# Four 128-row loads of wo in place of sixteen, and the last z1 load queued behind the fourth output store

## The chip, the cores and the metric

The kernel runs on one core of a Trainium2 chip. The metric is the device time of one execution in microseconds. Three runs of the kernel before gave 616.48, 617.76 and 618.69 us, with 617.76 us as the median.

## The reference

The input x (2048 tokens by 512 channels) goes through a layer norm without scale or shift. Two branches read the result, and x and both branches are added:

```
xn  = layernorm(x)
q, k, v = xn @ wqkv                      # 32 heads of 16
phi(t) = [softmax(t @ w_phi), softmax(-t @ w_phi)]
kv  = phi(k)^T v;  z = sum of phi(k) over the tokens
o   = phi(q) kv / (phi(q) z + 1e-6)      # linear attention
A   = o @ wo                             # wo is 512 x 512
z1, z2 = gelu(xn @ w_in) in two halves of 688 columns
g   = w_sp @ layernorm(z2) + b_sp        # w_sp is 2048 x 2048
B   = (z1 * g) @ w_out
out = x + A + B
```

## The kernel before

The tokens are split into 16 tiles of 128. Each product in full precision is made of three matrix multiplies: every operand is held as a rounded part (`_h`) and a rest (`_l`), and `mm3` (lines 55 to 59) issues high by high, high by low and low by high. A weight that comes from DRAM therefore passes two engines before it can be used: ACT rounds it (`round_h`, line 49) and DVE subtracts (`rest_l`, line 53).

The program has three stages. The first makes q, k, v, the softmax features and raw z1, and sends features (`e_d`) and raw z1 (`z1_d`) to DRAM. The second is the large product w_sp by layernorm(z2) (tiles `g`), two output tiles at a time; after each pair, `gate` multiplies by gelu(z1), turns the result on DVE and stores it (`u_d`, `ur_d`). The third, "the tail", is the loop of lines 1076 to 1104. For each pair of token tiles it does, on PE:

- `project_u` (line 1012): the gated tile `uh`, `ul` and its last rows `rt` times w_out, into `pout`;
- `attend` (line 995): the features `f` times `kvT`, into `po`; ACT and DVE then make the two parts of `oT` from `po`;
- `project_o` (line 1021): `oT` times wo (`woh`, `wol`), added into the same `pout`. ACT copies `pout` to `xr` (line 1040) and an accumulating store on POOL's queue adds it to `out` (line 1041);
- `attend_T` (line 976): for the pairs up to token tile 6, sixteen transposes on PE (line 989, into `ptq`) turn the features of the next pair; later pairs are turned by DVE and sent through DRAM (`q_d`).

`features(s)` normalises the features of tile s on DVE (`q_fin`, lines 564 to 571): a multiply and a reduce of 1,024 columns, four short instructions, and a second multiply of 1,024 columns on the tile `et`, which SP loads from `e_d` (line 557). The transposes for the pair (2, 3) need `features(2)` and `features(3)`.

The order around the change is that of the program as a scheduler laid it out. Each engine runs its instructions in order; a transfer is issued by an engine's queue in order too. SP's queue carries, before the tail: the features of the first pair (`f`, line 923), the gated tile 1 (`u`, lines 855 and 856), `kvT` (line 972), wo (line 850), then `et` of tile 3, the gated tiles 2 and 3 (`u`, `rt`), `et` of tile 4, and so on. POOL's queue carries the z1 loads (line 787), the stores of gated tiles (`u_d`, `ur_d`, lines 837 and 839), the feature stores (`q_d`, line 582; `qtmp` is their source in the tail) and the output stores. The queue instructions take their completion semaphores from a ring of eight, so that a load waits until the load eight places ahead of it on its queue has landed.

wo is used in an order of rows that suits `oT`: chunk c of 128 rows consists of four blocks of 32 rows, each 64 rows apart in DRAM. The kernel before loads the four blocks with four transfers:

```
    def load_w(src, parts, h, l, t):
        rows = 0
        for r0, r1 in parts:
            load_w.last = sp.dma_start(t[rows:rows + r1 - r0], src[r0:r1, :]).ins
            rows += r1 - r0
        return round_h(act, h, t[:rows]), rest_l(l, t[:rows], h)
```

The z1 of the last pair of tiles (14 and 15) is loaded at line 1097, in the turn i = 2 of the tail's loop, and is used by ACT's gelu (line 819) in the turn i = 6.

Of the kernel before, what the change touches and what calls it, by code (L numbers as in the profile page):

```python
# [10 lines left out]
F32 = mybir.dt.float32  # L11
F32R = mybir.dt.float32r
AF = mybir.ActivationFunctionType
ALU = mybir.AluOpType
# [4 lines left out]
P = 128  # L19
S, D, H, DH, FH = 2048, 512, 32, 16, 688  # L20
# [5 lines left out]
KF = FH // P  # L26
# [8 lines left out]
HP, QP = P // 2, P // 4  # L35
# [6 lines left out]
def mixer(ctx: ExitStack, tc: tile.TileContext, x, x_t, wv, wqkT, phi_bd, wo, w_in, wst, b_r, w_out, out):  # L42
    nc = tc.nc
    pe, act, dve, pool, sp = nc.tensor, nc.scalar, nc.vector, nc.gpsimd, nc.sync


    def round_h(eng, h, src):
        if eng is act:
            return act.activation(h, src, AF.Copy).ins  # L49
        return eng.tensor_copy(h, src).ins  # L50

    def rest_l(l, src, h, eng=None):
        return (eng or dve).tensor_tensor(l, src, h.bitcast(F32), op=ALU.subtract).ins  # L53

    def mm3(dst, a, b, start, stop):
        (ah, al), (bh, bl) = a, b
        pe.matmul(dst, ah, bh, start=start, stop=False)  # L57
        pe.matmul(dst, ah, bl, start=False, stop=False)  # L58
        return pe.matmul(dst, al, bh, start=False, stop=stop).ins  # L59
# [12 lines left out]
    def xz_tile(n, dt, name):  # L72
        return xz.tile([P, SL], dt, tag="xz", name=name)[:, :n]
# [121 lines left out]
    with ExitStack() as p0:  # L195
# [236 lines left out]
        t = xz_tile(2 * D, F32R, "xT").rearrange("p (a b) -> p a b", a=2)  # L432
# [8 lines left out]
        for cs, pt in zip(halves, pts):  # L441
            src = pt.rearrange("p a b -> p (a b)")
# [117 lines left out]
    def q_fin(et, tmp, zb):  # L560

        e, r, t, w = et[:, :NF], *(et[:, NF + k * 2 * H:NF + (k + 1) * 2 * H] for k in range(3))
        den = et[:, NF + 6 * H:QW]
        dve.tensor_tensor(tmp, e, zb, op=ALU.mult)
        dve.tensor_reduce(t, heads(tmp), axis=AX.X, op=ALU.add)
        dve.tensor_tensor(t, t, r, op=ALU.mult)
        dve.scalar_tensor_tensor(den, pairs(t, 0), EPS_DEN, pairs(t, 1), op0=ALU.add, op1=ALU.add)
        dve.reciprocal(den, den)
        dve.tensor_tensor(w.rearrange("p (h a) -> p h a", a=2), r.rearrange("p (h a) -> p h a", a=2),
                          den.unsqueeze(2).to_broadcast([P, H, 2]), op=ALU.mult)  # L570
        return e, dve.tensor_tensor(heads(e), heads(e), bc(w, 2 * H), op=ALU.mult).ins
# [6 lines left out]
    def turn_q(s, dst, e, eng):  # L578

        dve.transpose(dst.rearrange("p (m c t) -> p m c t", c=NB, t=BL), e.rearrange("p (c m j) -> p m c j", c=NB, j=BL))  # L580
        for b in range(P // BL):
            eng.dma_start(q_d[s, :, b * QB:(b + 1) * QB].rearrange("(m j) w -> j m w", j=BL),
                          dst[b * BL:(b + 1) * BL].rearrange("p (m w) -> p m w", w=QB))
# [154 lines left out]
    for s in range(NT):  # L738
# [4 lines left out]
        n = s // 2  # L743
# [3 lines left out]
        for k, q in p:  # L747
            ins = act.activation(z[(slice(None), *k)], q, AF.Gelu_apprx_tanh, scale=r_x[:, s:s + 1]).ins
# [6 lines left out]
        r = zw.tile([P, 1], F32, tag="rstd", bufs=2, name="rstd")  # L755
# [88 lines left out]
    def slot(name, dt=F32):  # L844
        return xz_tile(2 * FH, dt, name)

    def load_w(src, parts, h, l, t):
        rows = 0
        for r0, r1 in parts:
            load_w.last = sp.dma_start(t[rows:rows + r1 - r0], src[r0:r1, :]).ins  # L850
            rows += r1 - r0
        return round_h(act, h, t[:rows]), rest_l(l, t[:rows], h)

    def load_u(i, u, rt):
# [19 lines left out]
    lasts, wu = [None] * 9, []  # L874

    def stage_w():
        t = [xz2.tile([P, SL], F32, tag="b", name="wof") for _ in range(3)]
        w = [xz_tile(2 * D, F32R, "wu") for _ in range(KF + 1)]
        for c in range(KF + 1):
            n = P if c < KF else 2 * REM  # L880
            h, l = (w[c][:n, k * D:(k + 1) * D] for k in range(2))
            rows = [(c * P, (c + 1) * P)] if c < KF else [(KF * P, FH)] * 2
            load_w(w_out, rows, h, l, t[c // 2][:, c % 2 * D:(c % 2 + 1) * D])
            wu.append((h, l))

    g, es, ets, ft, brought = {}, {}, {}, {}, {}
    for n in range(NC):
# [4 lines left out]
        if n % NQ == NQ - 1 and i < NP - 1:  # L892
            c = gt.tile([P, 2, FU], F32, tag="c", name="c")
# [7 lines left out]
        if n % NQ == NQ - 1 and i < NP - 1:  # L901
# [3 lines left out]
            if i in (2, 4):  # L905
                s = i // 2 - 1
                e, t = (gt.tile([P, 2, FU], F32, tag=tag, name=name).rearrange("p k f -> p (k f)")[:, :NF]
                        for tag, name in (("c", "c"), ("z1", "z1t")))
                pool.dma_start(e, e_d[s, :, :NF])
                turn_q(s, t, e, pool)  # L910
        if n == NC - 4:
            stage_w()
# [6 lines left out]
        if n == NC - 2:  # L919
# [4 lines left out]
            t = xz_tile((KF + 1) * P, F32R, "u1")  # L924
# [9 lines left out]
    cw = ctx.enter_context(left("cw", 1))  # L934
# [7 lines left out]
    def er_pair(name):  # L942
        return cw.tile([P, 2, NF], F32, tag="er", bufs=3, name=name)

    def features(s):
        with tc.issue_after(fin[-1]):
            tmp = slot("qtmp")[:, :NF]
            es[s], ins = q_fin(ets.pop(s), tmp, zb)
        fin.append(ins)
        if s >= TQ:  # L950
            if s % 2 == 0:
                ft[s] = er_pair("f")
            turn_q(s, tmp, es.pop(s), pool)
            brought[s] = sp.dma_start(ft[s - s % 2][:, s % 2], q_d[s]).ins
            return
        lasts[6] = ins

    def gated(u):
        return split_u(*u, wk.tile([P, KF, P], F32R, tag="uh", name="uh"), wk.tile([P, KF, P], F32R, tag="ul", name="ul"))
# [2 lines left out]
    wo_h = cw.tile([P, ND, D], F32R, name="woh")  # L962
# [4 lines left out]
    wo_l = cw.tile([P, ND, D], F32R, name="wol")  # L967
# [53 lines left out]
    def project_o(i, oT, p):  # L1021
        ts = slice(i % 2 * P, (i % 2 + 1) * P)
        rows = slice(i * P, (i + 1) * P)
        xr = wk.tile([P, D], F32, tag="xr", bufs=3, name="xr")
        if i >= NT - 2:
            sp.dma_start(xr, x[rows, :])
        if i == NT - 1:
            dve.tensor_tensor(xr, p, xr, op=ALU.add)
            parts = [(slice(k * D // 2, (k + 1) * D // 2), pst.tile([P, D // 2], F32, tag="tr", name="pend")) for k in range(2)]
        else:  # L1030
            parts = [(slice(0, D), p)]
        for cs, q in parts:
            for c in range(ND):
                lasts[4] = mm3(q, (oT[0][:, c, ts], oT[1][:, c, ts]), (wo_h[:, c, cs], wo_l[:, c, cs]),
                               q is not p and c == 0, c == ND - 1)
            if i == NT - 2:
                dve.tensor_tensor(xr, p, xr, op=ALU.add)
                sp.dma_start(out[rows, :], xr)
            elif q is p:
                act.activation(xr, p, AF.Copy)  # L1040
                ins = pool.dma_start(out[rows, :], xr, accum_op=ALU.add).ins
                tc.add_manual_dep(ins, seeds[i].name, mybir.DependencyInfo(
                    mybir.DependencyClass.Sync, mybir.DependencyReason.DATA), reason="out holds x")
            else:
                dve.tensor_tensor(xr[:, cs], q, xr[:, cs], op=ALU.add)
                sp.dma_start(out[rows, cs], xr[:, cs])
# [7 lines left out]
    wk.tile([P, NG, 2 * P], F32R, tag="oTh", name="oT")  # L1054
    with tc.issue_after(lasts[0]), tc.issue_after(lasts[1]), tc.issue_after(fin[-1]):
        for c in range(ND):
            rows = [(m * QP, (m + 1) * QP) for m in range(c // 2 * 8 + c % 2, (c // 2 + 1) * 8, 2)]
            load_w(wo, rows, wo_h[:, c], wo_l[:, c], cw.tile([P, D], F32, tag="wof", bufs=4, name="wof"))
    with tc.issue_after(load_w.last):
        ets[3] = load_q(3, slot("et"))  # L1060
        for s in (2, 3):
# [14 lines left out]
    for i in range(0, NT, 2):  # L1076
        p[i] = project_u(i, nxt.pop(i))
        if 0 < i < NT - 2:
            nxt[i + 2] = gated(us.pop(i + 2))
        with tc.issue_after(lasts[2]):  # L1080
            oT = attend(fT)
        with tc.issue_after(lasts[3]):
            p[i + 1] = project_u(i + 1, nxt.pop(i + 1))
        if not i:
            fin.append(lasts[7])
            features(3)
            with tc.issue_after(fin[-1]), tc.issue_after(lasts[8]):
                nxt[2] = gated(us.pop(2))
        if i < NT - 2:
            with tc.issue_after(fin[-1]) if not i else ExitStack():  # L1090
                nxt[i + 3] = gated(us.pop(i + 3))
        for k in range(2):
            project_o(i + k, oT, p.pop(i + k))
            ahead(i + k)
        if i == 2:
            with tc.issue_after(lasts[6]):
                z = load_z1(NP - 1)
        if i == GATE_LAST:
            with tc.issue_after(lasts[0]), tc.issue_after(lasts[1]):
                gate(NP - 1, cb, z, z, gt.tile([P, 2, FU], F32, tag="zt", name="zt"))()  # L1100
            p2.close()
        if i + 2 < NT:
            with tc.issue_after(lasts[4]):
                fT = attend_T(i + 2)
# [33 lines left out]
```

## Time and profile before

| what | value |
|---|---|
| median of three runs | 617.76 us |
| time of the profiled execution | 615.26 us |
| its span, first to last instruction | 613.6 us |
| busy: PE, DVE, ACT, POOL | 606.3, 519.9, 259.9, 132.4 us |
| granted TensorE clock | 1.000 |
| moved by DMA | 107.85 MB, mean 176 GB/s |

The profile comes from one execution, 2.5 us below the median of the three runs; 1.7 us of its time lie outside its span. Times in its rows are microseconds from the start of the span. In a row of a timeline stand start, duration, engine, line, operation, result and operands; square brackets hold how long the engine had been idle and which event ended that. A DMA's "to landing" runs from its issue to its completion. In a row of the DMA queues stand packets, megabytes and the time that the packets took, as a share of 16 DMA engines over the window. In a row of the stretches stand the bounds, then busy times of PE, PEld, DVE, ACT and POOL with their counts, the granted clock, the mean share of the DMA engines, and GB/s.

### The profile page before, as it was taken

What the parts mean: (1) busy time and instruction counts of PE and PEld (TensorE: products, weight loads), DVE (VectorE), ACT (ScalarE), POOL (GpSimd) and SP (SyncE); (2) the same over time, 40 slices, a digit from 0 to 9 for tenths busy, and PEclk for the clock granted to TensorE, in tenths of its full rate; (3) what the DMA queues carried; (4) which work ended last, traced back from release to release, by engine and by line L of the source; (5) the groups of instructions that cost most, each with busy time, mean ns of one, the idle gap of its engine ahead of it and who ended that gap; (6) DMA issues with size and microseconds to landing.
All of it is one profiled execution on the core that took longest, in us unless ns stands there. A gap on an engine that the chain in (4) does not pass through costs nothing.

```text
span 613.6 us, 11385 instructions
## 1 busy us (share of the span) xinstructions
PE 606.3 (99%) x4286; PEld 551.5 (90%) x4286; DVE 519.9 (85%) x930; ACT 259.9 (42%) x414; POOL 132.4 (22%) x231
## 2 busy tenths in 40 slices
PE   8999999999999999999999999999999999999997
PEld 7888888888888999999999999999999978777776
DVE  5999999999988588999989897787779979999932
ACT  5653334423433547887434443332435243332220
POOL 4122232333111014542000002001100131053440
PEclk9999999999999999999999999999999999999999
DMA  8557776666547848001454746455566798599882
GB/s 309 196 135 170 224 174 183 153 161 171 134 120 206 275 155 308 2 1 35 150 135 133 193 100 182 132 158 145 162 179 215 239 312 253 150 293 278 222 221 67
DMA packets 57950, 107.85 MB, mean 176 GB/s; under 512 B 12392, under 2 KB 24552, under 8 KB 57672
## 3 DMA queue, kind: packets, MB, share of 16 engines
q1 hardware_dynamic: 43656, 65.22, 34.5%
q0 software_dynamic: 11936, 36.28, 24.0%
q10 hardware_dynamic: 2304, 5.64, 2.4%
q8 instruction: 33, 0.54, 0.4%
q14 instruction: 21, 0.17, 0.1%
HBM read 66.85 MB, written 35.54 MB: 167 GB/s over the span
## 4 chain that ended last, share of the span: by engine, by line
PE 83%; DVE 6%; DMA 6%; issue 2%; SPq 1%; ACT 1%; POOL 0%; ACTq 0%; DVEq 0%; POOLq 0%
PE g L57 8%; PE g L58 8%; PE g L59 8%; PE proj L58 7%; PE proj L57 7%; PE proj L59 7%; PE zps L58 6%; PE zps L59 6%; PE zps L57 6%; PE pout L57 5%; PE pout L59 5%; PE pout L58 5%; DVE A L53 2%; DMA wf<-in_wst 1%; PE po L1004 1%
## 5 line engine op out<-in xcount | busy, mean ns | idle before, releaser
L57 PE MATMUL g<-B,A 128*128 128x344 f32 x448 | 142.5, 319 | 0.3 <-DVE c L810 0.3
L58 PE MATMUL g<-B,A 128*128 128x344 f32 x448 | 142.4, 319 | 0.0
L59 PE MATMUL g<-B,A 128*128 128x344 f32 x448 | 138.9, 318 | 0.0
L57 PEld LDWEIGHTS g<-B,A 128*128 128x128 f32 x448 | 84.0, 188 | 0.9 <-DVE c L810 0.6
L58 PEld LDWEIGHTS g<-B,A 128*128 128x128 f32 x448 | 84.0, 188 | 0.0
L59 PEld LDWEIGHTS g<-B,A 128*128 128x128 f32 x448 | 83.6, 188 | 0.0
L49 ACT ACTIVATE A<-S 128x512 fp32r<-128x512 f32 x64 | 39.4, 628 | 70.7 <-DVE S L622 52.3
L57 PE MATMUL proj<-wqk_h,xT 128*128 128x512 f32 x128 | 50.1, 391 | 0.0
L59 PE MATMUL proj<-wqk_h,xT 128*128 128x512 f32 x128 | 49.8, 389 | 0.0
L58 PE MATMUL proj<-wqk_l,xT 128*128 128x512 f32 x128 | 49.8, 389 | 0.0
L125 ACT ACTIVATE e<-e,r_x 128x1024 f32<-128x1024 f32 x26 | 29.8, 1149 | 42.3 <-DVE e L124 41.3
L53 DVE TENSOR_TENSOR A<-S,A 128x512 fp32r<-128x512 f32 x64 | 43.0, 684 | 3.0 <-ACT A L49 2.8
L49 ACT ACTIVATE A<-wf 128x512 fp32r<-128x512 f32 (+1 forms) x64 | 32.8, 515 | 28.1 <-DMA wf<-in_wst 15.8
L57 PE MATMUL zps<-w1h,xT 128*128 128x344 f32 (+2 forms) x128 | 40.8, 320 | 0.0
L59 PE MATMUL zps<-w1h,xT 128*128 128x344 f32 (+2 forms) x128 | 40.7, 318 | 0.0
L58 PE MATMUL zps<-w1l,xT 128*128 128x344 f32 (+2 forms) x128 | 40.7, 318 | 0.0
L57 PE MATMUL zps<-w2h,xT 128*128 128x344 f32 (+2 forms) x128 | 40.7, 318 | 0.0
L58 PE MATMUL zps<-w2l,xT 128*128 128x344 f32 (+2 forms) x128 | 40.6, 317 | 0.0
L59 PE MATMUL zps<-w2h,xT 128*128 128x344 f32 (+2 forms) x128 | 40.3, 317 | 0.0
L53 DVE TENSOR_TENSOR A<-wf,A 128x512 fp32r<-128x512 f32 (+1 forms) x64 | 35.1, 550 | 4.1 <-ACT A L49 4.0
L787 POOL DMA_DIRECT2D z1t<-z_d x16 | 8.7, 550 | 132.5 <-DMA wf<-in_wst 98.1
L128 DVE TENSOR_REDUCE sm<-e 128x64 f32<-128x1024 f32 x26 | 31.1, 1199 | 2.5 <-ACT e L125 2.5
(219 smaller groups left out, 1434.4 us busy)
## 6 DMA issues: line engine op xcount, KB each, us to landing
wf<-in_wst SPq DMA_DIRECT2D x64, 256.0 KB, 3.4
e_d<-e POOLq DMA_DIRECT2D x16, 544.0 KB, 5.0
et<-e_d SPq DMA_DIRECT2D x16, 544.0 KB, 7.6
z_d<-z1f ACTq DMA_DIRECT2D x16, 344.0 KB, 3.1
z1t<-z_d POOLq DMA_DIRECT2D x16, 344.0 KB, 4.6
zacc<-e POOLq DMA_DIRECT2D x10, 512.0 KB, 4.8
u<-u_d SPq DMA_DIRECT2D x15, 320.0 KB, 5.8
xt<-in_x SPq DMA_DIRECT2D x16, 256.0 KB, 4.4
```

The costliest lines, as they stand in the source:

```text
L49: return act.activation(h, src, AF.Copy).ins
L53: return (eng or dve).tensor_tensor(l, src, h.bitcast(F32), op=ALU.subtract).ins
L57: pe.matmul(dst, ah, bh, start=start, stop=False)
L58: pe.matmul(dst, ah, bl, start=False, stop=False)
L59: return pe.matmul(dst, al, bh, start=False, stop=stop).ins
L125: softmax_pair.last = less, act.activation(e, e, AF.Exp, scale=scale).ins
L128: dve.tensor_reduce(sm, heads(e), axis=AX.X, op=ALU.add)
L787: pool.dma_start(t[:, k, :FH], z1_d[2 * i + k])
L1004: lasts[3] = pe.matmul(po[r][c * QP:(c + 1) * QP, k], kvT[rows, m // 2, cols], fs[m // 4][rows, m // 2 % 2], start=True, stop=True).ins
```

## The change

`load_w` takes a list of views of DRAM and issues one transfer for each. For wo, the four blocks of a chunk are one view of three dimensions (4 blocks, 32 rows, 512 columns), so that each chunk is one transfer of 128 rows. For w_out the transfers stay what they were. Besides, `lasts[6]`, behind which the last z1 load is put, is now the output store that was issued last and no longer the last instruction of `features`; at that place it is the store of output tile 3, the fourth.

```
-    def load_w(src, parts, h, l, t):
+    def load_w(parts, h, l, t):
         rows = 0
-        for r0, r1 in parts:
-            load_w.last = sp.dma_start(t[rows:rows + r1 - r0], src[r0:r1, :]).ins
-            rows += r1 - r0
+        for src in parts:
+            n = src.size() // D
+            load_w.last = sp.dma_start(t[rows:rows + n], src).ins
+            rows += n
         return round_h(act, h, t[:rows]), rest_l(l, t[:rows], h)
...
-        lasts[6] = ins
...
-                ins = pool.dma_start(out[rows, :], xr, accum_op=ALU.add).ins
+                lasts[6] = ins = pool.dma_start(out[rows, :], xr, accum_op=ALU.add).ins
...
-            rows = [(m * QP, (m + 1) * QP) for m in range(c // 2 * 8 + c % 2, (c // 2 + 1) * 8, 2)]
-            load_w(wo, rows, wo_h[:, c], wo_l[:, c], cw.tile([P, D], F32, tag="wof", bufs=4, name="wof"))
+            rows = wo[c // 2 * D // 2:(c // 2 + 1) * D // 2].rearrange("(m a r) d -> a m r d", a=2, r=QP)[c % 2]
+            load_w([rows], wo_h[:, c], wo_l[:, c], cw.tile([P, D], F32, tag="wof", bufs=4, name="wof"))
```

On SP's queue, ahead of the tail, stood the load of kvT, sixteen loads of wo (the staging tile is `wof`), and then the features of tile 3 and the gated tiles 2 and 3:

```order
L972 DMA kvT<-kvT_d 128x512
L850 DMA wof<-in_wo 32x512 x16
L557 DMA et<-e_d 128x1088
L855 DMA u<-u_d 128x640
L856 DMA rt<-ur_d 96x128
L855 DMA u<-u_d 128x640
L856 DMA rt<-ur_d 96x128
L557 DMA et<-e_d 128x1088
```

The same place now:

```order
L972 DMA kvT<-kvT_d 128x512
L851 DMA wof<-in_wo 128x1x512 x4
L557 DMA et<-e_d 128x1088
L856 DMA u<-u_d 128x640
L857 DMA rt<-ur_d 96x128
L856 DMA u<-u_d 128x640
L857 DMA rt<-ur_d 96x128
L557 DMA et<-e_d 128x1088
```

Twelve issues are gone ahead of the load of `et`; nothing else on SP has changed places here.

On POOL's queue, from the last z1 loads of the second stage to the first output stores of the tail, the order was this (`x6` holds the four loads of two earlier pairs and the two of the last pair):

```order
L787 DMA z1t<-z_d 128x688 x6
L837 DMA u_d<-z1t 32x8x160 x4
L839 DMA ur_d<-z1t 32x6x32 x4
L1041 DMA out<-xr 128x512 x4
L582 DMA q_d<-qtmp 32x4x256 x4
L1041 DMA out<-xr 128x512 x2
L582 DMA q_d<-qtmp 32x4x256 x8
```

The same place now:

```order
L787 DMA z1t<-z_d 128x688 x4
L837 DMA u_d<-z1t 32x8x160 x4
L839 DMA ur_d<-z1t 32x6x32 x4
L1041 DMA out<-xr 128x512 x4
L787 DMA z1t<-z_d 128x688 x2
L1041 DMA out<-xr 128x512
L582 DMA q_d<-qtmp 32x4x256 x4
L1041 DMA out<-xr 128x512
L582 DMA q_d<-qtmp 32x4x256 x8
```

The two loads of the last z1 have moved from ahead of the gated stores to behind the fourth output store, and the fifth output store now stands ahead of the first feature stores. PE's and ACT's orders are the same in both kernels. On DVE, in the tail, some instructions have changed places with their neighbours. The widest such move is at the two rests of `oT` of token tiles 6 and 7, which PE reads in `project_o`; before, both stood behind the last two long instructions of `features`:

```order
L567 SCALAR_TENSOR_TENSOR et<-et 128x32
L568 RECIPROCAL et<-et 128x32
L569 TENSOR_TENSOR et<-et 128x64
L571 TENSOR_TENSOR et<-et 128x1024
L564 TENSOR_TENSOR qtmp<-et,zb 128x1024
L53 TENSOR_TENSOR oT<-po,oT 128x2x256 x2
L580 STREAM_TRANSPOSE qtmp<-et 128x1024
```

The same place now:

```order
L568 RECIPROCAL et<-et 128x32
L569 TENSOR_TENSOR et<-et 128x64
L53 TENSOR_TENSOR oT<-po,oT 128x2x256
L571 TENSOR_TENSOR et<-et 128x1024
L564 TENSOR_TENSOR qtmp<-et,zb 128x1024
L53 TENSOR_TENSOR oT<-po,oT 128x2x256
L580 STREAM_TRANSPOSE qtmp<-et 128x1024
```

The first rest has moved ahead of these two; the second stands behind the same instructions as before.

More of the change, by code (lines that the diff above doesn't have):

```diff
@@ L881, in stage_w @@
             h, l = (w[c][:n, k * D:(k + 1) * D] for k in range(2))
-            rows = [(c * P, (c + 1) * P)] if c < KF else [(KF * P, FH)] * 2
-            load_w(w_out, rows, h, l, t[c // 2][:, c % 2 * D:(c % 2 + 1) * D])
+            rows = [w_out[c * P:(c + 1) * P]] if c < KF else [w_out[KF * P:]] * 2
+            load_w(rows, h, l, t[c // 2][:, c % 2 * D:(c % 2 + 1) * D])
             wu.append((h, l))
```

## The prediction

> **What bounds the kernel now.** I read the page's busy times first, then PE's waits, then the chain of waits around the only long one, then the timelines and DMA queues of that stretch. The page:
>
> ```profile
> span 613.6 us, 11385 instructions
> PE 606.3 (99%) x4286; PEld 551.5 (90%) x4286; DVE 519.9 (85%) x930; ACT 259.9 (42%) x414; POOL 132.4 (22%) x231
> ```
>
> PE is idle for 613.6 - 606.3 = 7.3 us in all, so no change that leaves its work alone can give more. PE's waits from 480 us to the end, where the change lies:
>
> ```profile
> PE ptq L989 <- DVE et L571: 1.0, 1, 1.0
> PE pout L57 <- ACT oT L49: 0.2, 1, 0.2
> PE pout L57 <- DVE c L810: 0.2, 1, 0.2
> ```
>
> The first two are within reach of the change: 1.0 + 0.2 = 1.2 us. Behind them PE has no gap until the last pair; the row of the stretches from 504 us shows 94.5 us busy in 94.5:
>
> ```profile
> 504.00:598.50 94.50, 94.50 (x597) 74.69 (x596) 82.52 (x124) 29.82 (x49) 29.02 (x45) 1.00 0.86 239
> ```
>
> So whatever PE gains or loses before 504 us arrives at the end of the kernel undiminished. The chain of waits shows what the 1.0 us hangs on (columns: start, duration, link):
>
> ```profile
> 480.17 6.96 DMA kvT<-kvT_d
> 487.14 0.31 SPq L850
> ...
> 492.24 6.33 DMA et<-e_d
> 498.58 1.24 DVE qtmp L564
> ...
> 502.24 1.24 DVE et L571
> 503.52 1.53 PE ptq L989 x12
> ```
>
> SP issues the sixteen wo loads one after another, held up by landings of earlier loads, and only then the `et` of tile 3. From its landing DVE needs 498.58 to 503.47 us, that is 4.9 us, and PE starts the remaining twelve transposes 0.05 us later. The other short wait belongs to wo itself, as the timelines of ACT, PE and DVE show:
>
> ```profile
> 495.09 0.63 ACT L49 ACTIVATE woh<-wof 128x512 fp32r<-128x512 f32 x1 [2.63 <-DMA wof<-in_wo]
> 496.26 0.50 PE L57 MATMUL pout<-woh,oT 128*128 128x512 f32 x1 [0.18 <-ACT oT L49]
> 496.36 1.28 DVE L53 TENSOR_TENSOR oT<-po,oT 128x512 fp32r<-128x512 f32 x2
> 501.89 0.60 PE L989 MATMUL ptq<-ident,et 128*128 128x128 f32 x4
> ```
>
> ACT is stuck on the last wo chunk until 495.09 us. Its two roundings of `oT` are queued behind that chunk, and so is PE's first product with wo, 1.17 us later. DVE's two rests of `oT` end at 496.36 + 1.28 = 497.64 us, 2.55 us after the landing, and `features(3)` follows them in DVE's order.
>
> **The change part by part: sixteen issues become four.** SP's row of the timeline:
>
> ```profile
> 480.60 11.54 SPq L850 DMA_DIRECT2D wof<-in_wo  x16
> ```
>
> On SP's queue this ends at 492.1 us. Four issues, each at up to 0.67 us (the longest of the `nm_d` issues quoted below, which also have more than two dimensions), end near 483.3 us, so `et` is issued some 9 us earlier. By itself this would take away the 1.0 us.
>
> **How fast the four loads run.** The source view now has 4 blocks as its outermost dimension; the blocks of before had 32 rows. The trace has one transfer whose outermost dimension is 4, the store of the turned means (`nm_d`, line 332), and here is the window that holds the packets of one such store, with its row by line, beside the page's rows of a 128-row store from ACT:
>
> ```profile
> q1 hardware_dynamic: 20, 0.00, 1.8%
> L332 SPq DMA_DIRECT2D nm_d<-mask x10: 508/529/665, 44.1 to 150.9; - x10
> ...
> q10 hardware_dynamic: 2304, 5.64, 2.4%
> z_d<-z1f ACTq DMA_DIRECT2D x16, 344.0 KB, 3.1
> ```
>
> Sixteen z1 stores leave 2304 packets, 144 each: 128 rows and 16 more. The `nm_d` store moves 4 x 4 runs of 32 floats, 16 packets, and leaves 20: only 4 more. I take the extra packets as one closing packet per DMA engine, so this transfer ran on 4 engines and the z1 stores on 16. The Trainium skill, page "DMA: Bandwidth & Descriptors", section "Why a DMA increments its semaphore by 16 and not by 1", states the rule behind it: a transfer is spread over the largest number up to 16 that divides the slowest dimension of both its sides. By this rule a wo load (4 blocks on one side, 128 partitions on the other) gets 4 engines; the trace agrees for 4 against 4, and no row has 4 against 128. The section "Rules for kernel authors" of the page warns against just such an outermost dimension.
>
> On 4 engines a load of 256 KB puts 65.5 KB on each, and the four loads follow one another on the same engines. The rate of one engine with 2 KB rows comes from two windows, the full queue of 5 to 12 us and the wo loads themselves, 487 to 490 us:
>
> ```profile
> q1 hardware_dynamic: 1407, 2.56, 98.4%
> ...
> q1 hardware_dynamic: 292, 0.39, 40.2%
> ```
>
> That is 2.56 MB in 0.984 x 16 x 7 = 110.2 engine-us, 23.2 KB per us, and 0.39 MB in 0.402 x 16 x 3 = 19.3, 20.2 KB per us. A load thus takes 2.82 to 3.24 us. I take 2.9, nearer the first, because four queued loads look like a full queue: 11.6 us for all (11.3 to 13.0).
>
> **When the wo loads start.** They run on their engines behind kvT, which landed at 487.1 us. Two z1 loads were in its way, and they move off:
>
> ```profile
> 479.41 1.07 POOL L787 DMA_DIRECT2D z1t<-z_d  x2 [23.89 <-DVE ul_rt L53]
> q0 software_dynamic: 160, 0.70, 49.1%
> wf<-in_wst SPq DMA_DIRECT2D x64, 256.0 KB, 3.4
> ```
>
> From 481.5 to 486 us POOL's queue took 49.1% of the engines, 4.5 x 0.491 = 2.2 us on each. Without it kvT lands at 484.9 us; the early end is its issue plus the median of the 64 loads of its size, 480.2 + 3.4 = 483.6. I take 484.2, near the middle.
>
> **What shares the four engines.** The gated stores go out on POOL's queue, between 490.5 and 499.5 us:
>
> ```profile
> q0 software_dynamic: 384, 0.75, 35.3%
> ```
>
> They take 9 x 0.353 = 3.2 us of each engine. About half of that falls before 496 us: 1.6 us (0 to 3.2).
>
> **The sum.** The last chunk lands at L = 484.2 + 11.6 + 1.6 = 497.4 us, where it landed at 495.09. `et` of tile 3, 544 KB over 16 engines, sits behind wo on those four with 34.8 KB, 1.5 to 1.7 us, so it is there by L + 1.7, before DVE is free at L + 2.55. The remaining transposes then start at L + 2.55 + 4.9 + 0.05 = L + 7.5, against 503.5 before. Equality lies at L = 496.0; at 497.4 the kernel loses 1.4 us. PE's wait for the first wo product grows from 0.2 to 497.4 + 1.17 - 496.08 = 2.5 us, and the one at the transposes shrinks to about 0.1. For L below 494.8 us both waits are gone, and the gain is 1.2 us and no more.
>
> **The z1 loads** cost nothing where they now stand:
>
> ```profile
> 520.53 0.86 POOL L1041 DMA_DIRECT2D out<-xr  x1 [0.78 <-ACT xr L1040]
> 535.84 0.60 POOL L582 DMA_DIRECT2D q_d<-qtmp  x1 [14.45 <-DVE qtmp L580]
> z1t<-z_d POOLq DMA_DIRECT2D x16, 344.0 KB, 4.6
> 546.53 1.34 ACT L819 ACTIVATE z1t<-z1t 128x1376 f32<-128x1376 f32 x1
> ```
>
> Issued behind the fourth output store, from about 521.4 us, two loads of 4.6 us have landed by 532, even if one waits for the other; gelu reads them at 546.5. POOL is idle there for 14.45 us, so nothing queues behind them. If that cover of 14 us were gone, gelu and the last gate would come later by what is missing. The fifth output store ahead of the first `q_d` store delays the latter by 0.9 us at most; POOL was waiting for DVE there. On DVE the second rest of `oT`, on which PE depends last, stands behind the same work as before, so the exchanged neighbours count nothing.
>
> **The rivals.** *All 16 engines carry the loads.* If the 128 partitions decide the spread, each load puts 16.4 KB on an engine and takes 0.7 us at 23.2 KB per us, and wo is there by 484.9 + 2.8 = 487.7 us. Both waits vanish: 1.2 us gained, 616.5 us. For it speaks that the destination has 128 rows; against it, the 20 packets. The same section of rules in the Trainium skill also advises joining loads under 64 KB into larger ones, and says such loads are mostly overhead; here the 64 KB loads of wo land in 2.0 to 5.4 us by their row, and 256 KB loads in 3.4, which agrees, if all engines take part:
>
> ```profile
> DMA to landing us min/median/max: 2.0/3.1/5.4
> ```
>
> *The gated stores take full turns on the four engines.* The mechanism is mine, its place the queues of these engines from 490 us: if kvT lands at its late end, 484.9, and all 3.2 us of POOL's packets come ahead of the last chunk, L = 484.9 + 11.6 + 3.2 = 499.7 and the loss is 3.7 us: 621.5. It decides from L = 497.9 on, where the loss passes 1.85 us. For it speaks that POOL issues these stores from 490.0 us on, while the wo loads are still running; against it, that a part of them lands later, the last issued ones at 494 + 5.8 = 500 us:
>
> ```profile
> 490.01 2.35 POOL L837 DMA_DIRECT2D u_d<-z1t  x4 [9.53 <-DVE z1t L833]
> 492.35 2.25 POOL L839 DMA_DIRECT2D ur_d<-z1t  x4
> ur_d<-z1t POOLq DMA_DIRECT2D x4, 24.0 KB, 5.8
> ```
>
> *The change gives nothing, because something else is late at 503.5 us.* DVE has been free there except for `et`, and SP's queue is the only thing ahead of it; I find no such thing and give this little.
>
> **How the numbers follow.** Added to the profiled execution's 615.26 us, 1.4 us gives 616.7; the median of the three runs is 617.76, so I predict 619.2. A measurement of this kernel can tell about 0.3%, 1.85 us, from no change, so the forecast itself counts as no change. Chances: four engines with L up to 497.9, 0.53; four engines with L later, the second rival among it, 0.30; all engines, 0.14; something else, 0.03. A gain over 1.85 us is beyond the 1.2 us at stake and could come only from scatter (the three runs span 2.2 us), mainly in the rival with all engines: 0.07. Slower takes the 0.30 and 0.02 of scatter: 0.32. The rest, 0.61, is no change. The range goes from 616.3 (1.2 us gained, 0.3 for scatter) to 621.5, the second rival's price.
>
> **What would show it right or wrong.** Right: four wo loads that land some 3 us apart, the last near 497.4 us; ACT's longest wait for `wof` just before it; PE's wait for `oT` near 2.5 us and that for `et` near zero. Fewer closing packets in the window of the wo loads (4 each, not 16) would show the spread. Wrong: wo landed by 488 us with both waits gone, or PE waiting for `et`, `u` or `z1t` at a place without a wait before.

## The result, and the profile after

The changed kernel takes 621.35 us (median of six runs, 620.49 to 622.78), the kernel before, measured beside it, 617.41 us (six runs, 616.15 to 618.69). The ratio is 1.0067, with a 95% interval of 1.0049 to 1.0086: 3.9 us slower. The forecast was 619.2 us and "no change"; the time lies in its range by 0.15 us, the sign went to the side that had a chance of 0.32.

The page of the changed kernel; its execution took 620.82 us:

```profile
span 619.1 us, 11365 instructions
...
PE 608.4 (98%) x4286; PEld 553.0 (89%) x4286; DVE 520.2 (84%) x930; ACT 260.2 (42%) x414; POOL 133.1 (22%) x231
...
q1 hardware_dynamic: 43416, 65.22, 34.6%
```

The span is 5.5 us longer. PE is idle for 10.7 us, 3.4 more than before, and busy for 2.1 us more with the same 4286 products. Queue q1 moves the same bytes in 240 fewer packets than before (43656). The sixteen wo loads left 16 x (32 + 16) = 768 packets; 528 are left, 4 x (128 + 4), so each load of 128 rows has four closing packets and ran on four engines.

PE's waits from 480 us to the end are down to one row:

```profile
PE pout L57 <- ACT oT L49: 4.3, 1, 4.3
```

The wait at the transposes (1.0 us before) is gone; the wait for the first wo product has grown from 0.2 to 4.3 us. The timelines of SP, ACT, PE and DVE around it:

```profile
481.90 2.42 SPq L851 DMA_DIRECT2D wof<-in_wo  x4
...
488.86 0.63 ACT L49 ACTIVATE woh<-wof 128x512 fp32r<-128x512 f32 x1 [3.53 <-DMA wof<-in_wo]
492.38 0.63 ACT L49 ACTIVATE woh<-wof 128x512 fp32r<-128x512 f32 x1 [2.88 <-DMA wof<-in_wo]
495.29 0.63 ACT L49 ACTIVATE woh<-wof 128x512 fp32r<-128x512 f32 x1 [2.28 <-DMA wof<-in_wo]
500.03 0.63 ACT L49 ACTIVATE woh<-wof 128x512 fp32r<-128x512 f32 x1 [4.11 <-DMA wof<-in_wo]
...
501.20 0.80 PE L57 MATMUL pout<-woh,oT 128*128 128x512 f32 x1 [4.27 <-ACT oT L49]
502.22 0.63 PE L57 MATMUL pout<-woh,oT 128*128 128x512 f32 x1
...
507.78 0.39 PE L58 MATMUL pout<-wol,oT 128*128 128x512 f32 x1
508.92 1.91 PE L989 MATMUL ptq<-ident,et 128*128 128x128 f32 x16
...
506.13 1.23 DVE L571 TENSOR_TENSOR et<-et 128x1024 f32<-128x1024 f32 x1
```

SP issues wo in 2.42 us instead of 11.54. The chunks land 3.5, 2.9 and 4.7 us apart, the last at 500.03 us where it had been there at 495.09, and PE's first product with it follows 1.17 us later, as before. But a product then takes 0.63 us in its row (0.43 from start to start), where a product of the same shape takes 0.39 (0.23) a few us later. The row of the stretches, cut at the changes of the granted clock, says why (columns: bounds, length, busy times of PE, PEld, DVE, ACT and POOL, granted clock, DMA share, GB/s):

```profile
495.52:498.93 3.41, 1.41 (x7) 0.82 (x5) 0.69 (x1) 0.40 (x1) 0.24 (x1) 1.00 0.96 338
498.93:502.34 3.41, 1.14 (x3) 0.95 (x4) 1.65 (x3) 1.78 (x4) 0.00 (x0) 0.50 0.42 137
502.34:505.75 3.41, 3.41 (x10) 2.64 (x9) 3.27 (x6) 1.30 (x2) 0.00 (x0) 0.50 0.82 262
505.75:509.17 3.42, 3.42 (x18) 2.77 (x17) 3.35 (x6) 0.65 (x2) 0.74 (x1) 1.00 0.91 309
512.00:604.50 92.50, 92.50 (x583) 72.94 (x583) 78.94 (x118) 27.75 (x45) 29.95 (x46) 1.00 0.85 230
```

PE's clock was halved from 498.93 to 505.75 us, 2.0 us after PE had run dry (501.20 - 4.27 = 496.93). Of those 6.83 us PE worked 4.55, so some 2.3 us of PE's time went into the slow clock. All six executions show a mean granted clock of 0.994 to 0.996, so it fell in each. Behind 512 us PE has no gap, so the delay arrives at the end undiminished: the transposes start at 508.92 us where they ended their wait at 503.52 before, 5.4 us later, and the span is 5.5 us longer. Of this, 0.9 us is not the change's: in this execution PE began its first `po` at 491.74 us, against 490.88 before, and SP issued kvT at 481.47, against 480.17, in a part where the queue and the products are the same. In the eleven profiles of this document kvT is issued between 479.60 and 481.92 us, so that much differs from one execution to the next.

The z1 loads are not late. POOL issues them, and gelu runs on time 25 us later:

```profile
526.87 1.45 POOL L787 DMA_DIRECT2D z1t<-z_d  x2
...
552.33 1.34 ACT L819 ACTIVATE z1t<-z1t 128x1376 f32<-128x1376 f32 x1
```

### The profile page after: what moved, and what is told of

Read it like the earlier page. It is cut to its first block, busy times and chain, and to the rows that moved or that the text cites. A ratio compares the mean times of both kernels' runs of the same rounds, so it can differ in the third digit from the quotient of the medians.

```text
span 619.1 us, 11365 instructions
## 1 busy us (share of the span) xinstructions
PE 608.4 (98%) x4286; PEld 553.0 (89%) x4286; DVE 520.2 (84%) x930; ACT 260.2 (42%) x414; POOL 133.1 (22%) x231
## 4 chain that ended last, share of the span: by engine, by line
PE 78%; DMA 7%; DVE 5%; issue 4%; POOL 3%; ACT 3%; SPq 0%; POOLq 0%; DVEq 0%; ACTq 0%
PE g L57 10%; PE g L58 10%; PE g L59 10%; PE proj L57 7%; PE proj L58 7%; PE proj L59 7%; PE pout L57 5%; PE pout L58 5%; PE pout L59 5%; DMA wof<-in_wo 3%; PE zps L58 2%; PE zps L59 2%; PE zps L57 2%; DMA z_d<-z1f 1%; DMA zacc<-e 1%
```

## The experiments

The theory after the result: wo is slow because four engines carry it, and that is the whole loss; its price at PE is the wait for the last chunk plus a halved clock that the wait brings on. Moving z1 is a gain, partly eaten. The rivals: that the order of the queues or the gated stores are the cause; that the z1 move does nothing; that the half clock costs nothing, because something else would be waited for.

**Only the z1 load moved.** Sixteen wo loads as before; the store of output tile 3 is what the last z1 load waits for:

```
-        lasts[6] = ins
...
-                ins = pool.dma_start(out[rows, :], xr, accum_op=ALU.add).ins
+                lasts[6] = ins = pool.dma_start(out[rows, :], xr, accum_op=ALU.add).ins
```

> The kernel before with the z1 load alone moved behind the fourth output store. Theory (four DMA engines carry the wo loads, and the z1 move only clears traffic ahead of them): kvT and the sixteen wo loads land 1 to 2 us earlier, PE's waits before 504 us shrink from 1.2 us towards 0, time 616.2 to 617.3 us against 617.4. Rival (the z1 loads at their new place delay the output stores, the loads of et and u, or gelu): 618.5 us or more, with a new wait of PE or ACT after 521 us.

Measured: 613.61 us (ten runs) against 617.29, ratio 0.9938 (0.9919 to 0.9958). ACT's and PE's timelines and the row of the stretches:

```profile
491.92 0.63 ACT L49 ACTIVATE woh<-wof 128x512 fp32r<-128x512 f32 x1 [3.34 <-DMA wof<-in_wo]
...
494.86 0.39 PE L57 MATMUL pout<-woh,oT 128*128 128x512 f32 x1
...
490.00:596.00 106.00, 106.00 (x677) 84.00 (x664) 90.95 (x137) 34.08 (x56) 35.34 (x55) 1.00 0.90 255
```

The last chunk is there 3.2 us earlier than before, PE begins its wo products without a wait and has no gap to the last pair. The direction was foreseen, the size was not: 3.7 us, three times the 1.2 us that the waits of the profile before had left to win (616.2 us was the lower end expected).

**Only the wo loads changed.** The changed kernel with the z1 load back ahead of the gated stores (the two lines above, reversed).

> The changed kernel with the z1 load back ahead of the gated stores, so that only the four wo loads are new. Theory: the z1 packets take 2.2 us of each engine ahead of wo again, the last wo chunk lands near 501.5 us and PE waits 5 to 6.5 us for it, time 622 to 624 us. Rival (the z1 move is what costs): 617.4 us, as before.

Measured: 622.52 us (six runs), ratio 1.0076 (1.0047 to 1.0106); the time as expected, the wait of 7.1 us above the 5 to 6.5. PE's wait, and two of the three stretches at half clock:

```profile
PE pout L57 <- ACT oT L49: 7.1, 1, 7.1
```

```profile
502.10:505.52 3.42, 1.86 (x4) 1.49 (x5) 2.37 (x4) 2.43 (x5) 0.00 (x0) 0.50 0.47 152
505.52:508.93 3.41, 3.41 (x9) 2.64 (x8) 3.20 (x7) 0.65 (x1) 0.00 (x0) 0.50 0.89 287
```

The loss stays without the z1 move, so it comes from the wo loads. In this profile the wait is 2.8 us longer than in the changed kernel's. In the times the z1 move is worth about 1 us there (622.5 against 621.35), which the two intervals do not tell from nothing.

**Four loads on sixteen engines.** The changed kernel, with wo passed in the order of its chunks, so that a load is a plain block of 128 rows:

```
-            rows = wo[c // 2 * D // 2:(c // 2 + 1) * D // 2].rearrange("(m a r) d -> a m r d", a=2, r=QP)[c % 2]
+            rows = wo[c * P:(c + 1) * P]
...
-        "wo": f(A_wo),
+        "wo": f(f(A_wo).reshape(2, 4, 2, QP, D).transpose(0, 2, 1, 3, 4).reshape(D, D)),
```

> The changed kernel, but wo is passed with its rows in the order of the chunks, so that each of the four loads reads 128 rows in one run and both its sides have 128 as the outermost dimension; the same bytes, the same four issues, the same places in the queues. Theory: each load closes with 16 small packets, wo has landed by 489 us, both waits of PE are gone, time 616.0 to 616.9 us. Rival (large loads in a row, or et behind them, are what is late): 620 us or more, and PE's wait for wo stays above 2 us.

Measured: 613.36 us (six runs), ratio 0.9929 (0.9903 to 0.9955), below the 616.0 to 616.9 us expected. Page, ACT and PE:

```profile
q1 hardware_dynamic: 43464, 65.22, 34.8%
...
485.63 2.52 ACT L49 ACTIVATE woh<-wof 128x512 fp32r<-128x512 f32 x4 [1.63 <-DMA wof<-in_wo]
...
495.21 0.39 PE L57 MATMUL pout<-woh,oT 128*128 128x512 f32 x1
```

There are 48 packets more than in the changed kernel, twelve closing packets for each of four loads: sixteen engines. All four chunks are rounded by 488.2 us, 7 us before PE wants them. Same bytes, same number of loads, same place on the queue: sixteen engines for four are worth 8.0 us (621.35 to 613.36). What else differs is that a load's 128 rows now lie together in DRAM; no run tests that by itself, but the run with two blocks to a load, below, goes by the engines.

**Sixteen engines, z1 left in its old place.** The kernel before with the four plain wo loads and nothing else; `lasts[6]` is set in `features`, as it was:

```
-            rows = [(m * QP, (m + 1) * QP) for m in range(c // 2 * 8 + c % 2, (c // 2 + 1) * 8, 2)]
+            rows = wo[c * P:(c + 1) * P]
```

> The kernel before with one edit: wo is passed in the order of its chunks, so that each chunk is one load of 128 whole rows (16 engines, four issues), and the load of the last z1 tiles stays where it was, ahead of the gated stores. The output is unchanged. Moving z1 alone gave 613.6 us and flat wo with z1 moved 613.4 us. Theory (the z1 load is what makes wo late in most executions, 16 issues or 4 make little difference): 616 to 617.5 us, at most 1.4 us below the kernel before. Rival (either of the two is enough to bring wo in ahead of the first wo product, since both end at the same floor): 613.4 to 614.5 us and no waits of PE behind 480 us.

Measured: 613.71 us (six runs), ratio 0.9939 (0.9919 to 0.9959). ACT's and PE's timelines:

```profile
488.64 2.60 ACT L49 ACTIVATE woh<-wof 128x512 fp32r<-128x512 f32 x4 [1.28 <-DMA wof<-in_wo]
...
496.31 0.39 PE L57 MATMUL pout<-woh,oT 128*128 128x512 f32 x1
```

The rival was right. Either half of the change, done without the loss of engines, brings wo in ahead of PE, and all three versions end at 613.4 to 613.7 us: there is one gain to be had here, and it is had once.

**Two blocks to a load.** The changed kernel with eight loads of two blocks of 32 rows (one run):

```
-            load_w([rows], ...)
+            load_w([rows[:2], rows[2:]], ...)
```

> The changed kernel with eight wo loads of two blocks of 32 rows each, so that the outermost dimension of the source is 2. Theory: each load runs on 2 engines, 32 rows on each; eight in a row need 256 rows of about 0.1 us on one engine, the last lands near 511 to 515 us, PE waits 15 to 19 us, and each load closes with 2 small packets; time 635 to 641 us. Rival (the number and size of the loads count, and not the outermost dimension): eight loads come out between four and sixteen, 617 to 621 us.

Measured: 632.35 us, below the 635 to 641 us of the theory and far above the rival's 617 to 621. Page and ACT's timeline:

```profile
q1 hardware_dynamic: 43416, 65.22, 34.0%
...
490.86 0.63 ACT L49 ACTIVATE woh<-wof 128x512 fp32r<-128x512 f32 x1 [5.54 <-DMA wof<-in_wo]
496.56 0.63 ACT L49 ACTIVATE woh<-wof 128x512 fp32r<-128x512 f32 x1 [5.07 <-DMA wof<-in_wo]
504.71 0.63 ACT L49 ACTIVATE woh<-wof 128x512 fp32r<-128x512 f32 x1 [7.52 <-DMA wof<-in_wo]
```

The 528 packets are now 8 x (64 + 2): two engines. The first three chunks land 5.7 and 8.2 us apart, PE waits 15.0 us. Halving the outermost dimension halves the engines; the loads are smaller, yet the whole is slower. So the spread goes by the outermost dimension. The Trainium skill, page "DMA: Bandwidth & Descriptors", section "Why a DMA increments its semaphore by 16 and not by 1", gives the rule for both sides of a transfer; 4 blocks against 128 partitions and 2 against 64 now agree with it.

**No gated stores beside the wo loads.** POOL's stores of gated tiles 12 and 13 are left out of the changed kernel, and those tiles are read from the place of 10 and 11, so that output tiles 12 and 13 are not the reference's:

```
-            eng = pool if i == NP - 2 else sp
+            if i == NP - 2:
+                return
+            eng = sp
...
-        sp.dma_start(u, u_d[i])
-        sp.dma_start(rt.bitcast(F32), ur_d[i])
+        j = i - 2 if i // 2 == NP - 2 else i
+        sp.dma_start(u, u_d[j])
+        sp.dma_start(rt.bitcast(F32), ur_d[j])
```

> The changed kernel without the gated stores of token tiles 12 and 13 (POOL's eight stores from 490 us on); the tail reads those of tiles 10 and 11 in their place, so output tiles 12 and 13 are left out. Theory: these packets take turns with wo on its four engines and cost the last wo chunk about 3 us; without them it lands near 497 us, PE waits 1 to 2 us, too short for the clock to fall, time 617.5 to 619.0 us. Rival (the four engines are slow by themselves): the last chunk lands at 499 us or later, PE waits over 3 us, time over 620.5.

Measured: 618.72 us (ten runs) against 617.54, ratio 1.0020 (0.9996 to 1.0044). ACT's and PE's timelines, and the one stretch at half clock:

```profile
488.52 0.63 ACT L49 ACTIVATE woh<-wof 128x512 fp32r<-128x512 f32 x1 [4.24 <-DMA wof<-in_wo]
491.43 0.63 ACT L49 ACTIVATE woh<-wof 128x512 fp32r<-128x512 f32 x1 [2.27 <-DMA wof<-in_wo]
495.08 0.63 ACT L49 ACTIVATE woh<-wof 128x512 fp32r<-128x512 f32 x1 [3.02 <-DMA wof<-in_wo]
498.15 0.63 ACT L49 ACTIVATE woh<-wof 128x512 fp32r<-128x512 f32 x1 [2.44 <-DMA wof<-in_wo]
...
499.32 0.50 PE L57 MATMUL pout<-woh,oT 128*128 128x512 f32 x1 [3.76 <-ACT oT L49]
```

```profile
499.92:503.33 3.41, 3.41 (x10) 2.63 (x9) 3.34 (x5) 1.48 (x2) 0.00 (x0) 0.50 0.81 250
```

The time is what the theory gave, the wait is not: 3.8 us, where it expected 1 to 2. Without any store beside them the last three chunks land in 9.63 us, 3.21 each, where the changed kernel's took 11.17: the stores cost these three 1.5 us, near the 1.6 us of the sum. (The landing itself is 500.03 - 498.15 = 1.9 us earlier, but SP also began to issue wo 1.4 us earlier in this execution, at 480.48 against 481.90; from that issue to the last chunk it is 17.67 us against 18.13, since the first chunk took longer here.) Four engines alone are late already. Yet the median is 2.6 us lower than the changed kernel's, two thirds of its loss, so the stores have their part in it. Seven of the ten executions show a mean granted clock of 0.996 or 0.997 and one 1.000, where five of the changed kernel's six show 0.994; in the profiles 0.997 is one stretch of 3.41 us at half clock and 0.994 two, so a stretch of half clock went with the stores in most executions.

**The clock kept up.** Eighteen unused 128x512 products in PE's gap ahead of the first wo product:

```
+        if not i:
+            t = pst.tile([P, D], F32, tag="tr", name="warm")
+            with tc.issue_after(lasts[2]):
+                for _ in range(18):
+                    w = pe.matmul(t, wu[0][0][:, :P], wu[0][0], start=True, stop=True, skip_group_check=True).ins
```

> The changed kernel with 18 idle products of 512 columns on PE (into a tile that nothing reads) between the last product with w_out of tile 1 and the first with wo, about the 4.3 us that PE stands still there. The wo loads land as before. Theory: the halved clock that followed the standstill is part of the loss; with PE kept busy the granted clock stays at 1.00, the products with wo run at 0.23 us each in place of 0.43, and the time falls by 1.5 to 2.3 us to 619.0 to 619.9. Rival (the loss is the late wo and et alone; the clock is made good by a later wait): 621.3 us.

Measured: 624.16 us (six runs), ratio 1.0101 (1.0073 to 1.0128), slower than the changed kernel. The stretches, and PE's timeline at a place that had no wait:

```profile
495.00:515.00 20.00, 19.89 (x121) 15.36 (x120) 14.26 (x21) 8.11 (x14) 3.31 (x5) 1.00 0.83 249
518.12:521.53 3.41, 1.43 (x7) 0.81 (x5) 3.41 (x4) 0.58 (x1) 0.00 (x0) 1.00 0.17 64
521.53:524.95 3.42, 2.57 (x6) 2.09 (x7) 3.32 (x9) 0.00 (x0) 0.00 (x0) 0.50 0.37 110
524.95:528.36 3.41, 3.41 (x9) 2.64 (x9) 3.34 (x4) 0.03 (x1) 0.00 (x0) 0.50 0.76 259
```

```profile
522.38 0.79 PE L59 MATMUL pout<-woh,oT 128*128 128x512 f32 x1 [2.83 <-DVE oT L53]
```

At its place the edit did what it should: full clock from 495 to 515 us. But the products also made the scheduler put DVE's rests of `oT` for tiles 2 and 3 behind `features(5)`, and PE waited there for 2.83 us, with a halved clock behind it. Its time therefore says nothing of the clock's price; its first pair, which lies ahead of that wait, is read below.

**The clock kept up, with DVE's order pinned.** Two kernels with the rests of a pair ahead of the features behind them, one without and one with fifteen such products:

```
-        with tc.issue_after(fin[-1]):
+        with tc.issue_after(fin[-1]), tc.issue_after(lasts[7] if s > 3 else fin[-1]):
```

> The control of the run with the unused products: the changed kernel with VectorE's order pinned in the same way (rests of oT of a pair ahead of the features behind them) and no unused products. The output is unchanged. Theory: that order is nearly what the changed kernel has anyway, so 621.3 us, at most 1 us to either side, with the clock halved behind the wait for the first wo product as in the changed kernel.

> The changed kernel with 15 unused 128x512 products (15 x 0.23 = 3.5 us of PE time) placed in PE's gap between project_u(1) and the first wo product, and with VectorE's order pinned so that the rests of oT of a pair stand ahead of the features behind them. The output is unchanged. My theory (PE's 4.27 us standstill halves the clock for 6.8 us, and the twenty-four wo products under it cost about 2.1 us): granted clock 1.00 throughout 495 to 515 us, first po to the first ptq 15.1 us, no halving later, and the time 2 us below the run beside it that has the same order without the products, that is about 619.2 us if that one is at 621.3. Rival (the half clock only hides work that would wait for something else anyway): 0 to 0.5 us below it.

Measured: 661.11 us (six runs, ratio 1.0714, 1.0689 to 1.0739) without the products, 656.42 us (six runs, ratio 1.0651, 1.0621 to 1.0680) with them. The expectation for the control failed: the pin holds back the features of the later pairs too, and PE waits 30 to 32 us for their loads (`f` from `q_d`) behind 545 us in both, so the two times cannot be read for the clock. The first pair, ahead of all that, can, since DVE's order there is the same in both. PE's timeline without the products, from the first `po` of one pair to that of the next, and the stretches:

```profile
490.59 1.09 PE L1004 MATMUL po<-f,kvT 64*32 64x256 f32 x32
...
500.33 0.50 PE L57 MATMUL pout<-woh,oT 128*128 128x512 f32 x1 [4.55 <-ACT oT L49]
...
507.53 1.69 PE L989 MATMUL ptq<-ident,et 128*128 128x128 f32 x14
...
513.25 1.09 PE L1004 MATMUL po<-f,kvT 64*32 64x256 f32 x32
```

```profile
494.07:497.48 3.41, 1.71 (x8) 1.08 (x6) 0.69 (x1) 0.63 (x1) 0.51 (x1) 1.00 0.96 344
497.48:500.89 3.41, 0.56 (x2) 0.49 (x3) 1.07 (x2) 1.60 (x3) 0.00 (x0) 1.00 0.35 128
500.89:504.31 3.42, 3.42 (x10) 2.63 (x9) 3.35 (x5) 1.48 (x2) 0.00 (x0) 0.50 0.78 230
```

And the same timeline with them:

```profile
491.89 0.88 PE L1004 MATMUL po<-f,kvT 64*32 64x256 f32 x24
...
496.92 3.61 PE L1096 MATMUL warm<-wu 128*128 128x512 f32 x15
500.68 0.50 PE L57 MATMUL pout<-woh,oT 128*128 128x512 f32 x1
...
506.66 2.10 PE L989 MATMUL ptq<-ident,et 128*128 128x128 f32 x16
...
512.58 1.09 PE L1004 MATMUL po<-f,kvT 64*32 64x256 f32 x32
```

The stretches with them:

```profile
495.00:515.00 20.00, 19.74 (x120) 15.06 (x119) 14.55 (x22) 8.81 (x15) 2.77 (x4) 1.00 0.84 262
```

The pair takes 512.58 - 491.89 = 20.69 us with the products, at full clock, and 513.25 - 490.59 = 22.66 without, 2.0 us more. From the first wo product to the transposes it is 5.98 against 7.20 us: 1.2 of the 2.0 us lie there, under the clock. The rest lies ahead of that product (8.8 against 9.7 us from the first `po`), in the landing of wo, which differs between any two executions. To leave the landing out, six profiles can be compared from ACT's rounding of the last chunk to the first `po` of the next pair, over which DVE's order is the same in all up to the features of tile 4: 13.07 and 13.08 us at full clock (eighteen and fifteen unused products), 14.09 and 14.13 with one stretch of 3.41 us at half clock (DVE's order pinned; no gated stores), 14.64 with two (514.67 - 500.03, the changed kernel) and 14.93 with three (only the wo loads). So the half clock costs 1.0, 1.6 and 1.9 us on PE's path; the rival that gave it 0 to 0.5 us is out.

## Why the prediction was wrong, step by step

**Right.** The spread over four engines and its sign in the packets; that the first wo product becomes the one that is late, with the wait at the transposes gone; what the gated stores add to the landing (1.6 us in the sum, 1.5 measured for three chunks); that the z1 loads have room where they now stand; that what is lost before 504 us arrives at the end.

**Wrong, the landing of the last chunk.** The step was "L = 484.2 + 11.6 + 1.6 = 497.4 us"; it landed at 500.03. The first chunk was there at 488.86 us instead of 484.2 + 2.9 = 487.1: 1.8 us, of which 1.3 are the later start of SP's queue in this execution. The other three took 11.2 us instead of 8.7 and the stores' 1.6: 0.9 us. The run without stores says which term it was: 3.21 us for a load, where 2.9 was chosen out of 2.82 to 3.24. "Nearer the first, because four queued loads look like a full queue" picked the wrong end: the rate that held, 65.5 KB in 3.21 us or 20.4 KB per us, is that of the wo loads of before (20.2), not that of the full queue (23.2). PE's wait for the first wo product became 4.27 us, not 2.5.

**Wrong, nothing in the sum spoke of the clock.** It let the transposes start when `et` is ready, L + 7.5. DVE kept to that (506.13 + 1.23 = 507.36 us, L + 7.3), but PE's own twenty-four products, at half clock in part, reached only to 508.92, so they came last by 1.5 us. At the 0.23 us of a product at full clock they would have ended by 501.20 + 5.6 = 506.8, ahead of `et`. The Trainium skill, page "TensorE: Matmul & The Clock Gate", section "Part 1: The HAM clock gate", tells of a clock gate that looks at PE's activity in free-running windows of 3413 ns and could have been weighed; the steps of 3.41 us in the traces agree with that window. Its warning against gaps over some 3.4 us would have let the predicted 2.5 us pass, and the traces here disagree with that bound: a standstill of 2.83 us was enough (below).

Inside the profiled executions the terms come to 1.4 us in the sum, 2.6 for the landing and 1.5 for the clock, 5.5 us; the span grew by 5.5. Without the 0.9 us by which PE came later to the tail, 4.6 us are left: the sum's 1.4, 1.7 for the landing (PE's wait grew by 1.8 over the forecast) and 1.5 for the clock. The medians differ by 3.9.

**Wrong, the offset from the profile to the median.** "1.4 us gives 616.7; the median of the three runs is 617.76, so I predict 619.2" carried the 2.5 us between the profiled execution of before and its median over to the new kernel. There it is 0.5 us (620.82 to 621.35). The profiled execution of before was one of its best. In differences, which need no such offset, 1.4 us were forecast and 3.9 measured; that 619.2 came nearer is luck: the errors of the sum, 4.1 us, less these 2.0 make the 2.1 us between 619.2 and 621.35.

**Wrong, the cap on a gain.** "The gain is 1.2 us and no more" was read from the waits of the same good execution. Three kernels with wo in time gained 3.5 to 3.9 us. In their profiles PE takes 106.6 us from the first `po` to that of the last pair, against 599.27 - 490.88 = 108.4 before: 1.8 us less, so the rows of waits understate even this execution by 0.6 us. For the rest, runs of the kernel before lie between 614.6 and 620.5 us, those of the three between 612.3 and 615.6. The granted clock of 38 further executions of before is on record: 18 show 0.994 to 0.997, one or two stretches of half clock by the measure above, where the profiled one shows 1.000; their median is 618.0 us, that of the other twenty 616.4. So in nearly half of its executions the clock falls, though the record does not say where in the kernel. Even the twenty lie 2.7 us above the three kernels, so they too probably wait longer for wo than the profiled one; no slower execution of before was profiled, and this part is argued and not shown.

The second rival gave 621.5 us and was closest in time, but not in its reason: it put 3.2 us of the landing on the stores, which cost the three chunks 1.5, and had no clock in it. That the range, which ends at its price, holds the result is luck too.

## What to carry to other kernels

Before joining loads, look at the outermost dimension of the joined view: with 4 or 2 blocks there the loads ran on four or two engines and the kernel lost, with 128 rows on sixteen and it gained. Here the blocks' order could be put into the data. A wait of PE is to be priced with the clock behind it: here that added 1.0 to 1.9 us to waits of 3.8 to 7.1 us. And a single profiled execution gives the place of a wait that hangs on a DMA, but no upper bound on what removing it gains; compare its time with the median first.

## What was unexpected of the hardware

In the traces the granted clock changed in steps of one period: the stretches of half clock behind a wait lasted 3.41, 6.83, 10.24 and 17.07 us, 1, 2, 3 and 5 times 3.41. Their rows above, cut at these steps, show what counts: a step in which PE was busy for 1.41 us (the changed kernel) or 1.43 (eighteen unused products) was followed by half clock, one with 1.71 us (DVE's order pinned) was not. At half clock, 1.86 and 2.57 us of work in a step did not bring the full clock back; a step full of work did. So about 2 us of standstill within one step were enough, and the standstill of 2.83 us brought half clock on. How much of a wait falls into one step depends on where the steps lie in that execution: the waits of 3.76 us (no gated stores) and 4.55 (DVE's order pinned) cost one step each, that of 4.27 between them (the changed kernel) two.

In these rows an engine's rate depended little on how many shared the load: two engines took 504.71 - 490.86 = 13.85 us for two chunks, 262 KB on each and 18.9 KB per us; four engines took 3.21 us for one, 65.5 KB on each and 20.4 KB per us, without the gated stores beside it (3.72 us and 17.6 KB per us with them).
